# Two loads of a fused attention and feed-forward kernel moved behind a wait on SyncE, and two norms moved ahead

## The chip, the cores and the metric

The kernel runs on one core of one Trainium2 chip. A core has five engines that run their own instruction streams in order: TensorE (PE, with its weight loads PEld), VectorE (DVE), ScalarE (ACT), GpSimd (POOL) and SyncE (SP). Here SP only issues transfers; POOL and ACT issue some too. All transfers run on the core's 16 DMA engines; those issued by SP appear in the profile as queue q1, those by POOL as q0. The metric is the device time of one launch in microseconds (us), lower is better.

## The reference

Cosine attention over 8 batches of 12 heads, 448 tokens, head size 64, and then a feed-forward layer over the joined heads (3584 tokens of 768 features, 2048 inner features):

```python
q_n = q / (np.linalg.norm(q, axis=-1, keepdims=True) + 1e-06)
k_n = k / (np.linalg.norm(k, axis=-1, keepdims=True) + 1e-06)
scores = np.matmul(q_n, k_n.transpose(0, 1, 3, 2)) / tau
scores = scores - np.max(scores, axis=-1, keepdims=True)
attn = np.exp(scores)
attn = attn / (np.sum(attn, axis=-1, keepdims=True) + 1e-09)
attn_out = np.matmul(attn, v)
...
h = x @ w_in
g = np.maximum(0.01 * h, h)
return (g @ w_out).astype(np.float32)
```

tau is 0.1; x is attn_out with the heads of a token side by side. Inputs and the output are float32.

## The kernel before

**Units of work.** Heads are taken two at a time: a *pair* s, numbered 0 to 47 over the whole problem, six pairs to a batch. A *double* j is two pairs (four heads), three to a batch. For each pair the kernel loads q and k (`load_qk`, four transfers on SP: q and k of the first 384 tokens, 192 KB each, and the remaining 64 tokens of each, 32 KB each), squares them on POOL (`squares`, L184), sums the squares on VectorE (`sums`, L195), takes roots on ScalarE (`roots`: a Ln and an Exp, L202 and L203), and scales q and k to bfloat16 `qn` on VectorE (`normalise`: add, reciprocal, two products at L219). `transposes` turns qn into `qkT`: for pairs 0 to 9 by seven matmuls on PE (L233) and a copy on VectorE (L257), from pair 10 on by a DMA transposition issued on SP (L251). `key_tiles` makes the scores of a pair in 128-key tiles on PE (L276) and their exps on ScalarE (`pe`, `pr`, L288). The softmax sums (`totals`) and the products with v (`products`) are matmuls too (L316, and L303 where two doubles share the rest of the keys); `reciprocals` and `scale` turn them into `xT`, the input of the feed-forward part.

**The feed-forward part** goes by chunks c, one to a batch: even chunks have 384 tokens and odd ones 512. `firsts` multiplies by w_in in 16 row tiles m of six matmuls each (L380), and ScalarE applies the leaky relu into `hT` (L387). `visit` multiplies by w_out (`two_groups`, L459): two output halves at once, two passes of 16 steps each, 32 steps n in all, two matmuls to a step; VectorE copies the two finished halves from PSUM to `osb` (L469) and SP stores them. Between the steps, at the numbers in `three` or `four`, a visit issues score tiles of the next batch, so ScalarE's exps run beside w_out's matmuls.

**Order of the work.** The whole order is written out by hand (`tc.manual_schedule()`): each engine executes its instructions in the order in which the Python code records them, and waits where data or a buffer is not ready. So an instruction that waits holds everything recorded behind it on its engine.

**The beginning.** Pairs 0 to 5 (batch 0) are loaded into `raw0` at once. `scaled(s)` at L577 scales pair s + 1, issues a `load_qk` for s = 0, 2 and 3 (pairs 7, 8 and 9; pair 6 is loaded just before, at L542), squares pair s + 3, and has POOL issue bulk transfers (`bulk`): v, four quarters of w_in (768 KB each: two halves of the inner features, and the even and the odd thirds of the model features), and w_out in two column halves, the first in two pieces of 768 KB and the second in four of 384 KB. A tiny copy on POOL (`hold`) makes POOL wait for a scaling before it goes on. Loads from pair 6 on go to the pool `ld` of four buffers, so pairs 6 to 9 have a buffer each, and load 10 waits for pair 6's.

**Pairs 6 to 11** (batch 1) are prepared while chunk 0 goes through w_in and w_out. `norm(s)` is roots, normalise, transposes, the next load, hold and the squares of pair s + 2. `norm(6)` and `norm(7)` are recorded ahead of `firsts(0, ...)`, which holds a table of what is recorded ahead of which m: the sums, norms and transposes of pairs 8 and 9 among them. Pairs 10 and 11 follow inside the first `visit`, at steps 4 and 20 of the first pair of output halves and step 4 of the second.

**PSUM** has eight banks, dealt by `banks`: the least recently used, alone or two side by side. A visit holds two of them for its output halves until VectorE has copied them, and deals the other six in twos to score tiles.

Of the kernel before, what the change touches and what calls it, by code (L numbers as in the profile page):

```python
# [16 lines left out]
def kernel(  # L17
# [10 lines left out]
    nc = tc.nc  # L28
# [89 lines left out]
    def main(x, b, h0, nh):  # L118
        return x[b, h0 : h0 + nh, 0:MAIN].rearrange("h (p t) d -> p h t d", t=3)
# [19 lines left out]
    def load_qk(s):  # L139
        if s >= NSLOT:  # L140
            return
        b, h0 = s // NPAIR, 2 * (s % NPAIR)
        both = ldp.tile([128, 2, 7, D], F32, name="qk")
        nc.sync.dma_start(out=both[:, :, 0:3], in_=main(q, b, h0, 2))
        nc.sync.dma_start(out=both[:, :, 4:7], in_=main(k, b, h0, 2))
        for i, x in enumerate((q, k)):
            nc.sync.dma_start(
                out=both[64 * i : 64 * i + 64, :, 3],
                in_=x[b, h0 : h0 + 2, MAIN:S].rearrange("h p d -> p h d"),
            )  # L150
        raw[s] = (both[:, :, 0:4], both[:, :, 4:7])
# [5 lines left out]
    def load_v(j):  # L157
        if j >= B * NQ:
            return
        b, jj = divmod(j, NQ)  # L160
        vb[j] = vbp.tile([128, 4, 3, D], BF16, name="v_b")
        gp.dma_start(out=vb[j], in_=main(v, b, 4 * jj, 4))  # L162
# [25 lines left out]
    def sums(s, parts=(0, 1)):  # L188
        if s >= NSLOT:
            return  # L190
        if s not in ss:
            ss[s] = smp.tile([128, 14], F32, name="ss")
        for i in parts:
            o = ss[s][:, 0:8] if i == 0 else ss[s][:, 8:14]
            nc.vector.tensor_reduce(  # L195
                o.rearrange("p (h t) -> p h t", h=2), sqs[s][i], axis=AX.X, op=ALU.add
            )
# [6 lines left out]
        if s < 2:  # L204
            nc.scalar.activation(ss[s], ss[s], func=AF.Identity, bias=eps)

    qn = {}

    def normalise(s):
        if s >= NSLOT:  # L210
            return
        r = smp.tile([128, 14], F32, name="r")
        if s >= 2:
            nc.vector.tensor_scalar_add(ss[s], ss[s], 1e-6)  # L214
        nc.vector.reciprocal(r, ss[s])  # L215
        qn[s] = qnp.tile([128, 7, 2, D], BF16, name="qn")
        for x, lo, hi, r0 in ((raw[s][0], 0, 4, 0), (raw[s][1], 4, 7, 8)):
            nt = hi - lo
            nc.vector.tensor_tensor(  # L219
                qn[s][:, lo:hi],  # L220
                x.rearrange("p h t d -> p t h d"),
                r[:, r0 : r0 + 2 * nt].rearrange("p (h t) -> p t h", h=2)
                .unsqueeze(3).to_broadcast([128, nt, 2, D]),
                op=ALU.mult,
            )
# [212 lines left out]
    def two_groups(c, two):  # L438

        po2 = banks(2, ("rows", c, two))
        last = {}
        for n in range(2):
            before, last = last, {}
            for m in range(MT):
                for h in range(2):
                    rows, i = slice(64 * h, 64 * h + 64), h ^ n
                    ts, half = two[i]
                    if n == 1 and m == 0:  # L450
                        tc.add_manual_dep(
                            nc.tensor.nop().ins,
                            before[i].ins.name,
                            mybir.DependencyInfo(
                                mybir.DependencyClass.Sync, mybir.DependencyReason.DATA
                            ),
                            reason="the other rows' products in this bank",
                        )
                    last[i] = nc.tensor.matmul(  # L459
                        out=po2[:, i, :HALF],  # L460
                        lhsT=hT[c][rows, m, ts * 128 : (ts + 1) * 128],
                        rhs=w_out_sb[rows, m, half * HALF : (half + 1) * HALF],
                        start=(n == 0 and m == 0), stop=(n == 1 and m == MT - 1),
                    )
                yield
        for i, (ts, half) in enumerate(two):
            if (c, ts) not in osb:
                osb[c, ts] = osp.tile([128, D_model], F32, name="osb")
            nc.vector.tensor_copy(  # L469
                out=osb[c, ts][:, half * HALF : (half + 1) * HALF], in_=po2[:, i, :HALF]  # L470
            )
            halves_done[c, ts] = halves_done.get((c, ts), 0) + 1
            if halves_done[c, ts] == 2:
                store(osb[c, ts], c, chunk_cols(c)[0] + ts * 128, 0, D_model)
        given_back(("rows", c, two))
# [101 lines left out]
    def scaled(s):  # L577

        if s and s + 2 < NPAIR:
            sums(s + 2, (0,))  # L580
        normalise(s + 1)
        if s != 1 and s < 4:
            load_qk(s + 7 - (s > 1))
        hold(qn[s + 1][:, 6, 0, 0:1])
        squares(s + 3)
        bulk(s)
        if s + 2 < NPAIR:
            sums(s + 2, (1,))
# [108 lines left out]
    def norm(s, transposed=True):  # L697
        if s >= NSLOT:
            return
        roots(s)  # L700
        normalise(s)
        if transposed:
            transposes(s)
        if 9 <= s < 12:
            load_qk(s + 2)
        elif s not in (7, 8):
            load_qk(s + 4)
        hold(qn[s][:, 6, 0, 0:1])
        squares(s + 2)
# [11 lines left out]
    def visit(b, order, norms, between):  # L721


        s0 = (b + 1) * NPAIR
        tiles = [(s0 + p, ki) for p in range(NPAIR) for ki in range(3)]
        key_tiles([(s0 + 1, 3), (s0 + 3, 3)])
        for i, two in enumerate(order):
            after = between[i == len(order) - 1]
            for n, _ in enumerate(two_groups(b, two), 1):
                for _ in range(after.get(n, 0)):  # L730
                    key_tiles([tiles.pop(0)])
                if not tiles and s0 + 5 not in ended:
                    ended.add(s0 + 5)
                    key_tiles([(s0 + 5, 3)])
                if n == 4 and i < norms:
                    norm(s0 + 4 + i)
                if n == 20 and i < norms - (b == 0):
                    sums(s0 + 5 + i)
        assert not tiles

    ended = set()
    three = ({5: 1, 11: 1, 16: 2, 21: 1, 27: 1}, {3: 1, 7: 1, 11: 1, 16: 2, 20: 1})
    four = ({5: 1, 11: 1, 16: 2, 24: 1}, {6: 1, 16: 2})
# [9 lines left out]
            8: [lambda: sums(9)],  # L753
            10: [lambda: norm(9, False), lambda: load_v(3)],
            11: [lambda: transposes(8), lambda: load_v(4)],
            13: [lambda: load_v(5), lambda: load_v_rem(1)],
            14: [lambda: transposes(9), lambda: sums(10)],
        },
    )
    ready = 10  # L760
    for b in range(B):
        tokens = chunk_cols(b)[1] // 128
        if b == B - 1:
            for ts in range(tokens):
                for half in range(2):
                    second(b, ts, half)
            break
        order = [((ts, 0), (ts, 1)) for ts in range(tokens)]
        if b == 0:
            order = [((0, 0), (1, 0)), ((2, 0), (0, 1)), ((1, 1), (2, 1))]  # L770
        visit(b, order, tokens - 1, three if tokens == 3 else four)
        ready += tokens - 1
        attend_batch(b + 1)
        for j in range((b + 2) * NQ, (b + 3) * NQ):
            load_v(j)
        load_v_rem(b + 2)
        s = ready
        between = {0: [lambda s=s: norm(s)], 1: [lambda s=s: sums(s + 1)]}
        if b == 0:
            between = {  # L780
                0: [lambda: sums(13)], 1: [lambda: norm(13), lambda: sums(14)],
                4: [lambda: norm(14), lambda: sums(15)], 7: [lambda: norm(15)],
                13: [lambda: sums(16)],
            }
            ready += 4
        elif tokens == 3:
            between.update({
                4: [lambda s=s: norm(s + 1), lambda s=s: sums(s + 2)],
                7: [lambda s=s: norm(s + 2), lambda s=s: sums(s + 3)],
                10: [lambda s=s: norm(s + 3)], 13: [lambda s=s: sums(s + 4)],  # L790
            })
            ready += 4
        else:
            between.update({
                4: [lambda s=s: norm(s + 1)], 5: [lambda s=s: sums(s + 2)],
                8: [lambda s=s: norm(s + 2)], 12: [lambda s=s: sums(s + 3)],
            })
            ready += 3
        firsts(b + 1, 0, between)
# [35 lines left out]
```

## Time and profile before

| | us |
|---|---|
| runs (median of 3) | 410.01 (409.76 to 410.94) |
| profiled execution, device time | 410.21 |
| its span | 408.4 |
| PE busy | 400.1 (98%) |
| ACT busy | 259.3 (63%) |
| DVE busy | 193.6 (47%) |
| POOL busy | 141.8 (35%) |

The times of the profile are microseconds from the start of its span. The granted clock of TensorE is full in the whole span. By the chain of work that ended last, 90% of the span lies on PE and 8% on transfers. The kernel's stages for batch 0 and chunk 0: attention from the start to about 30 us, w_in from 30.0 to 51.3, the first visit from 51.3 to 72.2, then attention of batch 1.

When transfers of the beginning were issued (their first issue), and when they had landed:

| transfer | issued | landed |
|---|---|---|
| load 8 (pair 8's q and k) | 16.21 | 28.5 |
| load 9 | 18.99 | 34.05 |
| load 10 | 38.38 | 48.2 |
| load 11 | 41.39 | 53.07 |
| w_in, four quarters | 15.45, 19.52, 22.99, 25.90 | 24.85, 30.66, 36.8, 40.4 |
| w_out, last piece | 33.26 | 60.06 |
| qkT of pair 10 | 56.26 | 65.4 |
| qkT of pair 11 | 60.99 | 68.3 |

A landing is the issue plus the time from issue to landing that the view of the DMA issues gives. Where a transfer's packets run and which ones alternate with them is seen in the same view, which counts packets and megabytes of each queue for any stretch.

### The profile page before, as it was taken

The page shows a single profiled execution, that of the slowest core. Times are in us where ns is not written, and L with a number is a line of the kernel's source. Part 1 is how long each engine was busy: PE and PEld are TensorE (multiplying, and loading weights), DVE is VectorE, ACT ScalarE, POOL GpSimd, SP SyncE. Part 2 cuts the span into 40 slices and gives each one's busy share as a digit, 9 for nine tenths or more (in the row PEclk, how much of TensorE's full clock was granted, in tenths as well). Part 3 has the DMA queues.
Part 4 walks back from the last instruction along what each step waited for, and adds up shares of the span by engine and source line. Part 5 has one row for each costly group of instructions (what it writes and reads, how often), then busy time and mean ns, then how long its engine had stood idle before and what let it go on. Part 6 is the DMA issues. An engine that isn't in the chain of part 4 may idle for free.

```text
span 408.4 us, 10108 instructions
## 1 busy us (share of the span) xinstructions
PE 400.1 (98%) x4096; PEld 212.5 (52%) x4096; DVE 193.6 (47%) x412; ACT 259.3 (63%) x448; POOL 141.8 (35%) x216
## 2 busy tenths in 40 slices
PE   7899999999999999999999999999999999999996
PEld 2335655444555655544555555544555555544564
DVE  6887951772644724355553635256262645130021
ACT  4996598455865579645875569745775559844300
POOL 4995473281323422253241614055231530000000
PEclk9999999999999999999999999999999999999999
DMA  8999999595495749378384857486376833210033
GB/s 184 252 220 210 222 191 195 179 204 125 119 212 85 143 90 216 64 116 161 95 205 100 124 134 153 122 116 136 90 192 128 125 75 63 63 41 2 0 77 79
DMA packets 104175, 54.21 MB, mean 133 GB/s; under 512 B 70016, under 2 KB 99072, under 8 KB 104128
## 3 DMA queue, kind: packets, MB, share of 16 engines
q1 hardware_dynamic: 78064, 41.04, 42.6%
q0 software_dynamic: 25216, 12.00, 23.3%
q8 instruction: 32, 0.52, 0.6%
q10 hardware_dynamic: 848, 0.52, 0.4%
q14 instruction: 15, 0.12, 0.1%
HBM read 45.61 MB, written 11.01 MB: 139 GB/s over the span
## 4 chain that ended last, share of the span: by engine, by line
PE 90%; DMA 8%; POOL 1%; SPq 1%; issue 0%; DVE 0%
PE ps L380 36%; PE ps L459 30%; PE ps L316 11%; PE ps L276 7%; PE ps L417 5%; DMA w_in_sb<-in_moe_w_in_dram 3%; DMA qkT<-qn 2%; DMA raw<-in_k_dram 1%; DMA raw<-in_q_dram 1%; PE ps L303 1%; DMA qk<-in_q_dram 1%; POOL sq L184 0%; PE ps L233 0%; POOL v_rem L169 0%; SPq L129 0%; SPq L134 0%
## 5 line engine op out<-in xcount | busy, mean ns | idle before, releaser
L380 PE MATMUL ps<-xT,w_in_sb 128*128 128x384 bf16 (+1 forms) x768 | 148.2, 353 | 0.4 <-DMA w_in_sb<-in_moe_w_in_dram 0.4
L459 PE MATMUL ps<-w_out_sb,hT 64*128 64x384 bf16 x1536 | 142.7, 323 | 0.0
L288 ACT ACTIVATE pe<-ps 128x896 bf16<-128x896 f32 x144 | 123.2, 918 | 20.0 <-PE ps L276 18.0
L387 ACT ACTIVATE hT<-ps 128x384 bf16<-128x384 f32 (+1 forms) x128 | 67.4, 543 | 70.2 <-PE ps L380 69.8
L380 PEld LDWEIGHTS <-w_in_sb 128*128 128x128 bf16 x768 | 74.1, 98 | 72.2 <-issue 4.0
L459 PEld LDWEIGHTS <-hT 64*128 64x128 bf16 x1536 | 73.6, 94 | 54.8 <-issue 3.3
L184 POOL TENSOR_TENSOR sq<-qk 128x512 f32<-128x512 f32 x84 | 77.5, 943 | 15.2 <-DMA qk<-in_k_dram 14.6
L469 DVE COPY osb<-ps 128x384 f32<-128x384 f32 x48 | 24.5, 553 | 77.8 <-PE ps L459 44.6
L276 PE MATMUL ps<-qkT 64*128 64x448 bf16 (+1 forms) x384 | 53.9, 354 | 2.0 <-ACT pe L288 0.9
L195 DVE TENSOR_REDUCE ss<-sq 128x6 f32<-128x384 f32 (+1 forms) x95 | 54.3, 610 | 1.2 <-POOL sq L184 1.0
L516 POOL CAST seen<-qn 128x1 f32<-128x1 bf16 x48 | 9.6, 199 | 130.5 <-DVE qn L219 125.9
L219 DVE TENSOR_TENSOR qn<-qk,r 128x512 bf16<-128x512 f32 x84 | 50.8, 646 | 2.0 <-DVE r L215 0.7
L214 DVE TENSOR_SCALAR ss<-ss 128x14 f32<-128x14 f32 x46 | 10.5, 229 | 66.9 <-ACT ss L203 66.9
L357 DVE TENSOR_TENSOR xT<-ps,rb 128x448 bf16<-128x448 f32 x48 | 27.8, 620 | 20.9 <-ACT rb L336 20.7
L162 POOL DMA_DIRECT2D v_b<-in_v_dram x24 | 18.8, 784 | 54.2 <-PE ps L316 54.2
L316 PE MATMUL ps<-pe,v_b 128*32 128x448 bf16 x576 | 31.9, 353 | 0.0
L276 PEld LDWEIGHTS <-qkT 64*128 64x128 bf16 (+1 forms) x384 | 16.5, 96 | 22.1 <-issue 8.8
L335 ACT ACTIVATE rb<-ps 128x448 f32<-128x448 f32 x24 | 12.9, 538 | 22.2 <-PE ps L316 21.2
L423 DVE COPY osb<-ps 128x384 f32<-128x384 f32 (+1 forms) x9 | 4.6, 513 | 36.6 <-issue 22.6
L288 ACT ACTIVATE pr<-ps 128x896 bf16<-128x896 f32 x24 | 21.3, 921 | 0.2 <-PE ps L276 0.2
L316 PEld LDWEIGHTS <-v_b 128*32 128x32 bf16 x576 | 15.0, 97 | 12.1 <-issue 0.6
L417 PE MATMUL ps<-w_out_sb,hT 128*128 128x384 bf16 (+1 forms) x144 | 21.0, 308 | 0.0
(51 smaller groups left out, 196.0 us busy)
## 6 DMA issues: line engine op xcount, KB each, us to landing
qk<-in_q_dram SPq DMA_DIRECT2D x42, 192.0 KB, 3.3
qk<-in_k_dram SPq DMA_DIRECT2D x42, 192.0 KB, 3.3
out_dram<-osb SPq DMA_DIRECT2D x30, 192.0 KB, 3.0
v_b<-in_v_dram POOLq DMA_DIRECT2D x24, 192.0 KB, 4.8
out_dram<-osb SPq DMA_DIRECT2D x12, 384.0 KB, 2.6
w_in_sb<-in_moe_w_in_dram POOLq DMA_DIRECT2D x4, 768.0 KB, 12.5
w_out_sb<-in_moe_w_out_dram POOLq DMA_DIRECT2D x2, 768.0 KB, 21.7
w_out_sb<-in_moe_w_out_dram POOLq DMA_DIRECT2D x4, 384.0 KB, 25.6
```

Source lines behind the costliest of these rows:

```text
L184: eng.tensor_tensor(sq, x, x, op=ALU.mult)
L195: nc.vector.tensor_reduce(o.rearrange("p (h t) -> p h t", h=2), sqs[s][i], axis=AX.X, op=ALU.add)
L219: nc.vector.tensor_tensor(qn[s][:, lo:hi], x.rearrange("p h t d -> p t h d"), r[:, r0 : r0 + 2 * nt].rearrange("p (h t) -> p t h", h=2) .u ...
L276: nc.tensor.matmul(out=out[:, a, :S], lhsT=x[rows, c0:c1], rhs=x[rows, 0:S], start=True, stop=True,)
L288: nc.scalar.activation(out=dst, in_=sc[:, :, :S], func=AF.Exp, scale=inv_tau)
L316: nc.tensor.matmul(out=x[32 * g : 32 * g + 32, :S], lhsT=weights(g, ki) if ki < 3 else rem(g), rhs=pe[s][:, ki, a, :] if ki < 3 else pr[j] ...
L357: nc.vector.tensor_tensor(xT[m][:, 2 * jj + e, half * S : (half + 1) * S], pos.pop((j, e))[:, :S], rbs[j], op=ALU.mult,)
L380: nc.tensor.matmul(out=pm[:, :n], lhsT=w_in_sb[:, kt, m * 128 : (m + 1) * 128], rhs=xT[c // 2][:, kt, c0 : c0 + n], start=(kt == 0), stop= ...
L387: nc.scalar.activation(out=hT[c][:, m, :n], in_=pms.pop((c, m))[:, :n], func=AF.Prelu, alpha=0.01)
L417: nc.tensor.matmul(out=po2[:, :n], lhsT=hT[c][:, m, ts * 128 : (ts + 1) * 128], rhs=w_out_sb[:, m, lo : lo + n], start=(m == 0), stop=(m = ...
L459: last[i] = nc.tensor.matmul(out=po2[:, i, :HALF], lhsT=hT[c][rows, m, ts * 128 : (ts + 1) * 128], rhs=w_out_sb[rows, m, half * HALF : (ha ...
L469: nc.vector.tensor_copy(out=osb[c, ts][:, half * HALF : (half + 1) * HALF], in_=po2[:, i, :HALF])
```

## The change

Four things are moved, and nothing is added to the arithmetic.

1. `load_qk(8)` and `load_qk(9)` leave `scaled(2)` and `scaled(3)` and stand in `scaled(4)`, behind an empty instruction on SP that waits for the second product of `normalise(5)`. The helper `behind` records such a wait; the one that `two_groups` already had on PE uses it now too, unchanged.
2. `transposes(9)` is recorded ahead of m = 13 in place of m = 14.
3. `norm(10)` is recorded ahead of m = 15 of `firsts(0, ...)` in place of step 4 of the visit's first pair of output halves.
4. `sums(11)` is recorded at step 16 in place of 20, and `norm(11)` at step 26 of the first pair of output halves in place of step 4 of the second. The other visits get the same steps as before, by a table.

The order of instructions on each engine: on PE the seven transposes of pair 9 pass six L380; on ScalarE the roots of pair 10 pass one hT and two pr, and the roots of pair 11 one exp; on VectorE the scaling of pair 11 passes the two copies of the first output halves. The orders on POOL and on SP are the same as before, except for the empty instruction on SP.

```diff
-    qn = {}
+    qn, scalings = {}, {}
+
+    def behind(eng, ins, why):
+
+        tc.add_manual_dep(
+            eng.nop().ins, ins.ins.name,
+            mybir.DependencyInfo(mybir.DependencyClass.Sync, mybir.DependencyReason.DATA),
+            reason=why,
+        )
...
-            nc.vector.tensor_tensor(
+            scalings[s] = nc.vector.tensor_tensor(
                 qn[s][:, lo:hi],
...
                     if n == 1 and m == 0:
-                        tc.add_manual_dep(
...
+                        behind(nc.tensor, before[i], "the other rows' products in this bank")
...
         normalise(s + 1)
-        if s != 1 and s < 4:
-            load_qk(s + 7 - (s > 1))
+        if s == 0:
+            load_qk(7)
+        elif s == 4:
+            behind(nc.sync, scalings[5], "weights first")
+            load_qk(8)
+            load_qk(9)
         hold(qn[s + 1][:, 6, 0, 0:1])
...
-                if n == 4 and i < norms:
-                    norm(s0 + 4 + i)
-                if n == 20 and i < norms - (b == 0):
-                    sums(s0 + 5 + i)
+                for fn in norms.get((i, n), ()):
+                    fn()
...
-            13: [lambda: load_v(5), lambda: load_v_rem(1)],
-            14: [lambda: transposes(9), lambda: sums(10)],
+            13: [lambda: load_v(5), lambda: load_v_rem(1), lambda: transposes(9)],
+            14: [lambda: sums(10)],
+            15: [lambda: norm(10)],
...
-        visit(b, order, tokens - 1, three if tokens == 3 else four)
+        norms = {(0, 16): [lambda: sums(11)], (0, 26): [lambda: norm(11)]}
+        if b:
+            norms = {}
+            for i in range(tokens - 1):
+                norms[i, 4] = [lambda s=ready + i: norm(s)]
+                norms[i, 20] = [lambda s=ready + i + 1: sums(s)]
+        visit(b, order, norms, three if tokens == 3 else four)
```

## The prediction

> **What bounds the kernel now.** First the waits of TensorE between 24 and 75 us, in total, times and longest:
>
> ```profile
> PE ps L380 <- DMA w_in_sb<-in_moe_w_in_dram: 0.4, 1, 0.4
> PE ps L276 <- DMA qkT<-qn: 0.3, 1, 0.3
> ```
>
> Two transfers stop TensorE. The timeline (start, length, engine, group, idle before it) gives their places:
>
> ```profile
> 30.01 0.34 PE L380 MATMUL ps<-xT,w_in_sb 128*128 128x384 bf16 x1
> 30.70 0.66 PE L380 MATMUL ps<-xT,w_in_sb 128*128 128x384 bf16 x3 [0.36 <-DMA w_in_sb<-in_moe_w_in_dram]
> 65.44 0.36 PE L276 MATMUL ps<-qkT 64*128 64x448 bf16 x2 [0.32 <-DMA qkT<-qn]
> ```
>
> Idle time understates such a wait, since matmuls are pipelined; starts are better. The second L380 starts 0.69 after the first where the stage runs at 0.16 (96 in 15.71): 0.53 us lost on the second quarter of w_in. For qkT I compare the same stage of two batches, stretches of 51.36 to 72.19 and 146.91 to 167.00:
>
> ```profile
> 51.36:72.19 20.83, 20.44 (x248) 11.09 (x254) 6.66 (x14) 18.91 (x26) 10.98 (x15) 1.00 1.29 186
> 146.91:167.00 20.09, 20.09 (x249) 11.26 (x253) 7.22 (x16) 18.91 (x26) 4.79 (x7) 1.00 0.59 121
> ```
>
> The first number is length, the second PE busy: visit 0 is 0.74 longer than visit 2. Before 30 us ScalarE is the limit (busy 9.55 and 9.82 of the 10 us from 10 and from 20) and the loads gate nothing there; after 72 us PE meets no wait that the list shows. So the change can win at most 0.53 + 0.74 = 1.27 us, 0.31%.
>
> **Part 1: loads 8 and 9 behind a wait on SP.** Nothing is added but one empty instruction. SP's next work, load 10, waits for the scaling of pair 6 until 38.38 (a wait of 16.1 us in SP's list), so SP has room: pair 5 is scaled by 27.45 (L219 at 26.29, 1.16), the eight issues at about 0.6 end by 32.3. POOL's weight queue (q0) is not passed or held. In the present run loads 8 and 9 are issued from 16.21 and 18.99, and their packets alternate one for one with q0's:
>
> ```profile
> q0 software_dynamic: 158, 0.32, 89.4%
> q1 hardware_dynamic: 143, 0.08, 19.2%
> ...
> q0 software_dynamic: 320, 0.24, 75.9%
> q1 hardware_dynamic: 316, 0.23, 46.6%
> ```
>
> (packets, MB, share; first two lines 20 to 22 us, beside w_in; the others 42 to 44, beside w_out.) A w_in quarter of 384 packets lands 3.6 us after the one before when it is alone (36.8, 40.4), so 9.4 ns a packet; 158 such packets leave 0.5 us of two for q1's 143, some 3.5 ns each. The second quarter lands at 30.66 with about 1,000 q1 packets interleaved ahead of it, so without them between 27 and 28; it is needed at 30.17. Gain 0.53, with at least 2 us of cover.
>
> Price: loads 8 and 9 land later. From first issue to last landing, the loads of before take 12.3 (load 8), 15.1 (9), 9.8 (10) and 11.7 us (11). Load 9 is now issued from 29.9, so it lands between 41.6 (11.7) and 45.0 (15.1). I take 44.0: the first packet moves 3.6 us after the issue, as load 10's did (38.38, then 4 packets until 42.0), so at 31.1; w_in is through at about 35.6, some 380 packets later, and the remaining 1,150 of the two loads' 1,536 go at 160 per us beside w_out until 42.7, plus 1.3 to landing as for loads 10 and 11. Load 8 by the same count lands at 39.3; POOL wants it at 38.1, and waits. Load 10 follows load 9 in the queue: 48.7 (47.7 to 49.9), against 48.2 now.
>
> **Part 2: the transposes of pair 9 one chunk earlier.** This costs PE nothing in work (7 matmuls, 0.39 either way), but they move ahead of six L380, and what they read is barely ready now:
>
> ```profile
> 41.66 1.04 POOL L184 TENSOR_TENSOR sq<-qk 128x512 f32<-128x512 f32 x1
> 45.43 1.14 DVE L195 TENSOR_REDUCE ss<-sq 128x8 f32<-128x512 f32 x2
> 47.67 1.16 DVE L219 TENSOR_TENSOR qn<-qk,r 128x512 bf16<-128x512 f32 x2
> 48.86 0.55 PE L233 MATMUL ps<-id,qn 128*128 128x128 bf16 x7
> ```
>
> These are pair 9's squares (first half), sums, scaling and transposes. The scaling ends at 48.83; the chain has the transposes at 49.02. The new place is 49.02 − 6 × 0.1625 − 0.53 = 47.5, done at 47.9 if the data were there. It isn't: if all of VectorE's work moved up by the same 0.53, the scaling would end at 48.30. With load 9 at 44.0 the squares end at 45.85 (1.82 both), and by the rows above the scaling ends 2.83 after the squares (second sum 0.57, then 48.83 − 46.57 = 2.26), at 48.65. Three transposes remain, 0.2: PE is through at 48.85, 0.95 late. Bounds: 0.6 (load 9 before 43.6) and 1.95 (at 45.0). PE takes matmuls in order, so all of w_in's last chunks wait behind it. This gives back more than part 1 gains; without part 1's 0.53 the wait would be 0.4 and the sum the same.
>
> **Part 3: pair 10's norm ahead of the visit.** The roots (0.55 of ScalarE) stand before the last hT and the two pr instead of behind them. They need sums(10), which end 2.76 after load 10 lands (48.37, 51.13): 51.45 by my 48.7, and ScalarE comes free at 51.35 (hT at 50.42 + 0.49, plus PE's 0.42). So almost no wait; the last hT ends about 52.6, and the bank it frees is wanted by the scores of the visit's fifth step at 53.1. Cover 0.5; past it each us costs one. Pair 10's transposition is issued near 54.0 instead of 56.26 and takes 9.1 at most as now: 63.1, wanted at 65.4. Gain 0.48 (start 65.44 against 64.96 by the steps of 0.081).
>
> **Part 4: pair 11's norm at the 26th step.** On ScalarE this passes one exp only (0.82): the roots start at 58.2 to 58.7 with PE's delay, against 58.63, the transposition at 60.5 against 60.99. Load 12 is now issued 2 to 3 us sooner, so less stands ahead of it; at 7.3 us as now it lands at 67.8, wanted at 68.1. Gain the other 0.26. Against it, VectorE evicts the first two output halves (2 × 0.51) behind the norm, until 61.4 instead of 59.37; the dealing order gives their banks to the second pair's 16th step, on PE at 61.12 + 0.42 = 61.54. It just fits; I take 0, with 0.5 as the bad end.
>
> **Sum**: −0.53 + 0.95 − 0.74 = −0.3 us (bounds −0.7 and +0.7 with load 9's). The profiled execution has a span of 408.4 within 410.21; it becomes 408.1 within 409.9. The median of the runs, 410.01, becomes **409.7**.
>
> **The rivals.**
> *Load 9 lands late (slower).* Place: PE stands at L233 for pair 9 (L219 late). The break-even is a wait of 1.27, load 9 at 44.3, only 0.3 past my estimate; each us more costs one. At 45.0, the longest latency of before, 410.7; load 10 at 49.9 then holds the roots on ScalarE until 52.65, hidden behind PE's own delay. Slower by 1.2 us needs 45.6. For it: q1 gets one packet per w_in packet, and both loads now queue right behind each other; against: w_in is through sooner. The Trainium skill (DMA: Bandwidth & Descriptors, Rules for kernel authors) advises to issue a DMA early, compute, and wait on it late. This change does the reverse for these two loads, and by that rule this rival would be the outcome; the trace agrees as far as load 8 lies landed for 10 us (28.5 to 38.6) now.
> *The whole gain (faster).* Pair 9 is scaled by 47.5 and nothing else waits: −1.27, 408.7. For it: the scaling of pair 7 takes 2.63 (38.70) instead of 1.16 beside POOL's squares(8), and a later load 8 would part them. Against: then squares(8) themselves, until 41.1, set sums(8), now at 41.24.
> *A later wait takes the gain.* The evictions of part 4 come 0.5 late, or the last piece of w_out (lands 60.06, read at 60.47) is pushed back by pair 10's transposition, whose packets now share its last 2 us: +0.5 on my sum, 410.2.
> *The change doesn't free w_in*: the second quarter stays late. Then 0.53 is lost, but the wait in part 2 shrinks by as much: 409.7 again.
>
> **How the numbers follow.** Forecast (with the last rival) 0.46, late load 0.31, later wait 0.1, whole gain 0.13. The measurement can tell about 0.3% (1.2 us) from no change. Faster by that needs nearly the whole cap: 0.14 with the edge of the forecast. Slower by that is two thirds of the late-load case, since its queue carries load 10 along, and a little of the later waits: 0.24. The rest is 0.62. The range leaves out the top of the late case and the edge of the whole gain: 408.8 to 411.2; the likeliest case alone has 409.3 to 410.7.
>
> **What would show it.** Right: no PE wait on w_in at 30; an idle of PE at pair 9's transposes near 48, released by DVE L219; POOL idle before squares(8) and (9) for DMA qk; no PE wait on qkT; visit 0 near 20.1 us. Wrong: no idle at L233 (then the whole gain), or one of over 2 us, or ScalarE idle before L202 near 51 with PE held behind it at L276.

## The result, and the profile after

The changed kernel took 412.44 us (median of 9 runs, 411.19 to 413.96) against 410.01 us before (9 runs, 409.70 to 411.15). The ratio is 1.0057, with a 95% interval of 1.0035 to 1.0079: slower, by about 2.4 us where 0.3 us less was forecast, and above the top of the range (411.2). The nine runs fall in two groups: five between 411.19 and 412.44, with a mean granted clock of 1.000, and four between 413.29 and 413.96, with 0.996. The profiled execution is one of the first group: 411.59 us, span 409.8.

The changed kernel's lines from L207 on carry other numbers: pair 9's scaling is L227 (L219 before), the transposes L241 (L233), scores L284 (L276), w_in L388 (L380), hT L395 (L387), w_out L460 (L459), the DMA transposition L259 (L251). "Before" is the kernel before throughout.

Waits of TensorE between 24 and 75 us, in the changed kernel (total, times, longest):

```profile
PE ps L241 <- DVE qn L227: 2.1, 1, 2.1
```

Both waits of before, for w_in and for qkT, are gone from that list, and one new wait stands there that is larger than what they were worth. The timeline of the changed kernel (start, length, engine, group, idle before it and what ended it), first TensorE:

```profile
30.18 0.82 PE L388 MATMUL ps<-xT,w_in_sb 128*128 128x384 bf16 x4
...
45.73 1.95 PE L388 MATMUL ps<-xT,w_in_sb 128*128 128x384 bf16 x11
49.76 0.81 PE L241 MATMUL ps<-id,qn 128*128 128x128 bf16 x7 [2.08 <-DVE qn L227]
```

At 30.18 four L388 run without a gap, so the 0.53 us of the second quarter of w_in is won. At 47.68 TensorE has done what stands before pair 9's transposes and then does nothing for 2.08 us. What it waits for begins on SP, whose timeline in the changed kernel has the four issues of load 9:

```profile
29.99 0.60 SPq L144 DMA_DIRECT2D qk<-in_q_dram  x1
30.64 0.47 SPq L145 DMA_DIRECT2D qk<-in_k_dram  x1
31.15 2.60 SPq L147 DMA_DIRECT2D qk<-in_q_dram  x1
33.80 1.24 SPq L147 DMA_DIRECT2D qk<-in_k_dram  x1
```

The timeline of POOL and VectorE in the changed kernel has the squares of pairs 8 and 9, and the second pair's sums and scaling:

```profile
40.60 1.83 POOL L184 TENSOR_TENSOR sq<-qk 128x512 f32<-128x512 f32 x2 [2.35 <-DMA qk<-in_k_dram]
45.49 1.82 POOL L184 TENSOR_TENSOR sq<-qk 128x512 f32<-128x512 f32 x2 [2.94 <-DMA qk<-in_k_dram]
46.56 1.34 DVE L195 TENSOR_REDUCE ss<-sq 128x8 f32<-128x512 f32 x2 [0.76 <-POOL sq L184]
49.01 1.16 DVE L227 TENSOR_TENSOR qn<-qk,r 128x512 bf16<-128x512 f32 x2
```

The four issues of load 9 run from 29.99 to 35.04; the last landed 11.5 us after 33.80, at 45.3. POOL stands idle for load 8 (until 40.60) and then for load 9 (until 45.49), VectorE for POOL, and the scaling ends at 50.17: 1.34 later than before, and TensorE wants it 1.5 sooner. Loads 8, 9, 10 and 11 landed at 40.4, 45.3, 50.25 and 55.2: a train, 5 us to a pair. The DMA view says why it is no faster. Packets, MB and share of each queue of the changed kernel from 34 to 36 us, and from 38 to 40:

```profile
q0 software_dynamic: 165, 0.33, 86.3%
q1 hardware_dynamic: 164, 0.11, 23.7%
...
q0 software_dynamic: 339, 0.26, 82.6%
q1 hardware_dynamic: 345, 0.17, 42.5%
```

The loads' queue (q1) gets as many packets as POOL's (q0) and no more: 82 per us while q0 carries packets of 2 KB, some 170 when they are of 768 bytes. A pair has 768 packets, so at 155 per us it takes 5 us.

The visit itself, from 53.49, where the chain of work that ended last reaches its first scores (51.36 before; stretch, length, then busy time and instructions of PE, PEld, DVE, ACT and POOL, granted clock, DMA share, GB/s):

```profile
53.49:73.58 20.09, 20.09 (x249) 11.24 (x254) 6.50 (x14) 18.62 (x24) 10.57 (x15) 1.00 1.12 174
```

It is 20.09 long, as long as visit 2, where nothing waits: the 0.74 us is won too. The books of the profiled execution: the visit starts 2.13 later than before (53.49 against 51.36) and is 0.74 shorter, so 1.4 us are lost, and the span grew by 1.4 (408.4 to 409.8). Of the 2.13, 0.17 lie ahead of w_in, whose first matmul starts at 30.18 instead of 30.01. That much is no effect of the change: among the profiles below, two kernels whose order up to there is that of before start w_in at 29.80 (parts 3 and 4 alone) and at 31.05 (part 4 alone). What follows the visit takes 336.3 us in every profile.

### The profile page after: what moved, and what is told of

It is laid out like the page before. It is cut to its first block, busy times and chain, and to the rows that moved or that the text cites. A ratio compares the mean times of both kernels' runs of the same rounds, so it can differ in the third digit from the quotient of the medians.

```text
span 409.8 us, 10098 instructions
## 1 busy us (share of the span) xinstructions
PE 400.0 (98%) x4086; PEld 212.9 (52%) x4096; DVE 191.9 (47%) x412; ACT 259.0 (63%) x448; POOL 140.3 (34%) x216
## 3 DMA queue, kind: packets, MB, share of 16 engines
q1 hardware_dynamic: 78064, 41.04, 43.2%
## 4 chain that ended last, share of the span: by engine, by line
PE 87%; DMA 6%; DVE 2%; SPq 2%; issue 1%; POOL 1%; ACT 0%; POOLq 0%
PE ps L388 32%; PE ps L460 31%; PE ps L324 10%; PE ps L284 7%; PE ps L425 5%; DMA qk<-in_k_dram 3%; DMA raw<-in_k_dram 2%; PE ps L311 1%; DVE qn L227 1%; DMA raw<-in_q_dram 1%; SPq L147 1%; POOL sq L184 1%; DMA qk<-in_q_dram 1%; DVE ss L195 0%; DVE ss L222 0%
## 5 line engine op out<-in xcount | busy, mean ns | idle before, releaser
L388 PE MATMUL ps<-xT,w_in_sb 128*128 128x384 bf16 (+1 forms) x760 | 147.6, 352 | 0.4
L460 PE MATMUL ps<-w_out_sb,hT 64*128 64x384 bf16 x1536 | 142.8, 323 | 0.0
L395 ACT ACTIVATE hT<-ps 128x384 bf16<-128x384 f32 (+1 forms) x128 | 67.2, 543 | 70.0 <-PE ps L388 69.5
L388 PEld LDWEIGHTS <-w_in_sb 128*128 128x128 bf16 x768 | 74.1, 98 | 71.7 <-issue 4.0
L460 PEld LDWEIGHTS <-hT 64*128 64x128 bf16 x1536 | 73.6, 94 | 54.9 <-issue 3.3
L184 POOL TENSOR_TENSOR sq<-qk 128x512 f32<-128x512 f32 x84 | 76.6, 933 | 19.1 <-DMA qk<-in_k_dram 18.4
L284 PE MATMUL ps<-qkT 64*128 64x448 bf16 (+1 forms) x384 | 53.9, 354 | 1.8 <-ACT pe L296 0.9
L227 DVE TENSOR_TENSOR qn<-qk,r 128x512 bf16<-128x512 f32 x84 | 49.0, 625 | 2.0 <-DVE r L223 0.6
L284 PEld LDWEIGHTS <-qkT 64*128 64x128 bf16 (+1 forms) x384 | 16.5, 96 | 21.1 <-issue 8.8
```

Of the source, the lines that this page charges most:

```text
L184: eng.tensor_tensor(sq, x, x, op=ALU.mult)
L227: scalings[s] = nc.vector.tensor_tensor(qn[s][:, lo:hi], x.rearrange("p h t d -> p t h d"), r[:, r0 : r0 + 2 * nt].rearrange("p (h t) -> p ...
L284: nc.tensor.matmul(out=out[:, a, :S], lhsT=x[rows, c0:c1], rhs=x[rows, 0:S], start=True, stop=True,)
L388: nc.tensor.matmul(out=pm[:, :n], lhsT=w_in_sb[:, kt, m * 128 : (m + 1) * 128], rhs=xT[c // 2][:, kt, c0 : c0 + n], start=(kt == 0), stop= ...
L395: nc.scalar.activation(out=hT[c][:, m, :n], in_=pms.pop((c, m))[:, :n], func=AF.Prelu, alpha=0.01)
L460: last[i] = nc.tensor.matmul(out=po2[:, i, :HALF], lhsT=hT[c][rows, m, ts * 128 : (ts + 1) * 128], rhs=w_out_sb[rows, m, half * HALF : (ha ...
```

## The experiments

The twelve experiments ran on three chips, four to a chip in the order below, each beside runs of the kernel before on the same chip: 410.49 us on the first (18 runs), 409.84 on the second (12) and 410.13 on the third (35). Ratios are against those, with 95% intervals.

### Parts 2 to 4 without part 1

```diff
-        if s == 0:
-            load_qk(7)
-        elif s == 4:
-            behind(nc.sync, scalings[5], "weights first")
-            load_qk(8)
-            load_qk(9)
+        if s != 1 and s < 4:
+            load_qk(s + 7 - (s > 1))
```

> Loads 8 and 9 back in their old places, the rest of the change kept. Theory A (load 9 lands at 45.4 and PE stands at pair 9's transposes for its scaling): load 9 lands near 34 again, pair 9 is scaled by 48.8, and PE idles about 0.7 us at the transposes instead of 2.1; the wait on w_in (0.5 us lost) returns and the 0.74 us of the visit stay won: 409.9, all runs within 1 us of each other. Theory B (the reordering costs by itself: the roots of pair 10 ahead of the last hT, the scaling of pair 11 ahead of the evictions): still near 412.

Measured: 411.7 us (411.15 to 412.02), 1.0030 [1.0018, 1.0041]. The wait for pair 9's scaling shrank as theory A has it, to 0.38, but the time hardly did. TensorE's timeline shows a wait that no theory named:

```profile
48.44 0.81 PE L241 MATMUL ps<-id,qn 128*128 128x128 bf16 x7 [0.38 <-DVE qn L227]
69.80 0.55 PE L284 MATMUL ps<-qkT 64*128 64x448 bf16 x4 [1.19 <-DMA qkT<-qn]
```

Pair 11's qkT was issued sooner than before (60.70 against 60.99) and landed later, at 69.75 instead of 68.3. So the late load 9 is one cause and not the only one. Theory B named this time, but not this place: TensorE's list has no wait behind the last hT or behind the copies of the output halves. What moves pair 11's transposition is parts 3 and 4, which are taken alone below.

### Part 2 taken back

```diff
-            13: [lambda: load_v(5), lambda: load_v_rem(1), lambda: transposes(9)],
-            14: [lambda: sums(10)],
+            13: [lambda: load_v(5), lambda: load_v_rem(1)],
+            14: [lambda: transposes(9), lambda: sums(10)],
```

> The transposes of pair 9 back ahead of m = 14; loads 8 and 9 stay behind the wait, the norms stay early. Theory A: pair 9 is scaled at 50.2 as in the changed kernel, PE comes to the transposes one chunk (0.98 us) later, so it idles 1.1 instead of 2.1 and the time falls by 1.0: span 408.8, time about 410.5, with fewer runs above 413. If the place of the transposes is the whole cause: no idle at L241, 409. Theory B: no change, 412.

Measured: 411.22 us (410.21 to 412.65, 11 runs), 1.0015 [1.0001, 1.0030], the smallest loss of any version with the train of loads, and near the 0.5 us over the kernel before that theory A expected. The wait for the scaling is 0.83 in place of 2.08 (1.1 was expected). Now the other edge of the change shows, the roots of pair 10 on ScalarE ahead of the last hT:

```profile
53.99 0.36 PE L284 MATMUL ps<-qkT 64*128 64x448 bf16 x2 [0.53 <-ACT hT L395]
```

So the earlier place of the transposes turns lateness of the data into idle time of TensorE; it doesn't make the data late.

### The two loads behind an earlier scaling

```diff
-        elif s == 4:
-            behind(nc.sync, scalings[5], "weights first")
+        elif s == 3:
+            behind(nc.sync, scalings[4], "weights first")
```

> SyncE waits for pair 4's scaling (24.0) in place of pair 5's (27.6), the rest of the change kept. Theory A: loads 8 and 9 land 1.5 to 3 us sooner (load 9 at 42.5 to 44), PE idles 0.5 to 1.2 us at pair 9's transposes, no wait on w_in at 30: 409.3 to 410. If instead the loads can't get through before w_in has landed wherever they are issued: load 9 lands less than 0.7 us sooner, idle over 1.5, 411. Theory B: 412.

Measured: 411.79 us (411.29 to 412.54), 1.0037 [1.0023, 1.0051]. The last issue of load 9 was at 28.78 instead of 33.80, five us sooner, and it landed at 43.4 instead of 45.3, two sooner: the queue sets the landing more than the issue does. The wait at the transposes is 0.3, less than the 0.5 to 1.2 expected, but 1.5 us appear at the scores of pair 11 (qkT issued at 60.07, landed 9.35 later). The expected 409.3 to 410 was a miss, by the same second wait as without part 1.

### The idle time filled

Nine matmuls on constant data (2.1 us) stand before pair 9's transposes; the rest is the changed kernel.

```diff
-        tp = transposed()
+        bank = banks(1)
+        if s == 9:
+            for i in range(9):
+                nc.tensor.matmul(
+                    out=bank, lhsT=warm[:, :128], rhs=warm, start=(i == 0), stop=(i == 8)
+                )
+        tp = bank.bitcast(BF16)[:, : 7 * 128].rearrange("p (t c) -> p t c", c=128)
```

> The changed kernel with nine matmuls on constants (9 x 0.216 = 1.9 us) in front of pair 9's transposes, into the bank that the transposes then overwrite, so that PE works where it stood idle. Theory C (the runs of the changed kernel near 413.5, all with a mean clock of 0.996, are those in which TensorE's clock is lowered after the idle of 2.1 us): span within 0.3 of the changed kernel's 409.8, clock 1.0 in every run, all runs between 411.0 and 412.2. Theory D (those runs come from the transfers): still some four of nine above 413.

Measured: 411.83 us (411.49 to 412.19), 1.0034 [1.0022, 1.0046]. With 2.1 us of matmuls added the time is that of the changed kernel's first group, so those us were free. None of its 6 runs has a clock under 0.999, where 4 of 9 of the changed kernel had 0.996.

### Part 1 alone

The order on all engines is that of before, except that loads 8 and 9 are behind the wait for the sixth pair's scaling:

```diff
-        if s != 1 and s < 4:
-            load_qk(s + 7 - (s > 1))
+        if s == 0:
+            load_qk(7)
+        elif s == 4:
+            behind(nc.sync, scalings[5], "weights first")
+            load_qk(8)
+            load_qk(9)
```

> Only part 1: loads 8 and 9 behind the wait on pair 5's scaling, transposes and norms in the order of before. Theory A (load 9 late, pair 9 scaled near 50): PE idles 0.8 to 1.2 us at L241, and pair 10, whose load follows at 50.3, is transposed late as well, so PE waits again at qkT: 411 to 411.7. If the late loads cost nothing without the moved transposes: 409.5.

Measured: 411.48 us (410.54 to 412.27), 1.0037 [1.0023, 1.0051], as expected. The wait at the transposes in their old place:

```profile
50.27 0.81 PE L241 MATMUL ps<-id,qn 128*128 128x128 bf16 x7 [0.97 <-DVE qn L227]
```

The expected second wait, at pair 10's qkT, didn't come, so the time was right partly by luck. The span of the profiled execution is 0.9 above before, but 0.8 of this lies ahead of w_in (30.82 against 30.01), where profiles of kernels alike up to there differ as much. From w_in to the end of the visit this profile is only 0.1 longer than before: no wait for w_in, the wait of 0.97, and a visit that begins late and is 0.75 shorter. The medians differ by 1.6. So the loss of part 1 alone is shown by the times; this profile shows the late load but not where most of the 1.6 us go.

### Parts 3 and 4 alone

Here and in part 4 alone, the lines taken out are the order of before, written with the change's table.

```diff
+            15: [lambda: norm(10)],
...
-        norms = {(0, 4): [lambda: norm(10)], (0, 20): [lambda: sums(11)], (1, 4): [lambda: norm(11)]}
+        norms = {(0, 16): [lambda: sums(11)], (0, 26): [lambda: norm(11)]}
```

> Only parts 3 and 4: norms of pairs 10 and 11 early, loads and transposes of before. Theory E (found in the first runs: with pair 10's transposition and load 12 issued sooner, their packets push those of v back, and pair 11's transposition, though issued sooner, shares the engines with v and lands near 69.7 in place of 68.3): no wait at qkT of pair 10, but 1.5 to 2 us at qkT of pair 11, span near 409.6, time 411 to 411.7. If the norms win what the prediction gave them (0.74): 409.3.

Measured: 411.63 us (411.38 to 412.93), 1.0045 [1.0032, 1.0058], as theory E expected. The two moves meant to shorten the visit lengthen it when nothing delays TensorE before it. The profile is of the slowest of the six runs (412.93, span 411.2), in which the clock falls as well after the wait, as the last section shows. In TensorE's timeline:

```profile
69.57 0.55 PE L284 MATMUL ps<-qkT 64*128 64x448 bf16 x4 [2.00 <-DMA qkT<-qn]
```

### Part 1 alone, behind the earlier scaling

The edit is that of part 1 alone, with `scalings[4]` at s = 3.

> Part 1 alone with the wait on pair 4's scaling: load 9 lands near 43.4, pair 9 is scaled in time for transposes at their old place, no wait on w_in. Theory F (what PE gains at 30 us it gives back at the next wait for a transfer, since qkT of pair 10 lands when the transfers allow): wait at qkT of pair 10 near 0.8 in place of 0.3, time within 0.3 of before. If the 0.53 us stay won: 0.5 below before.

Measured: 412.12 us (410.18 to 412.88, 7 runs), 1.0044 [1.0028, 1.0061]: a miss. The wait for the scaling is gone, and two others stand in its place, first the last piece of w_out (issued at 32.97, landed 28.9 later, at 61.9), then qkT:

```profile
61.89 0.81 PE L460 MATMUL ps<-w_out_sb,hT 64*128 64x384 bf16 x7 [1.12 <-DMA w_out_sb<-in_moe_w_out_dram]
70.34 0.55 PE L284 MATMUL ps<-qkT 64*128 64x448 bf16 x4 [1.12 <-DMA qkT<-qn]
```

In this profile w_out's last piece is later than in any other. That the loads' packets made it late is not shown: with loads 8 and 9 both behind a wait it landed between 59.9 (the changed kernel) and 61.9, in the other kernels between 60.0 and 60.5. Only here did TensorE come for it sooner than it landed.

### The changed kernel again

> The changed kernel once more, on the chip of this call. Theory A and C: near 1.0057 of before, part of its runs about 2 us above the rest with a mean clock below 1.0, and the idle of PE at L241 over 2 us. If the high runs belong to the first chip alone: all runs within 1 us.

Measured: 412.76 us (410.97 to 414.01), 1.0064 [1.0041, 1.0087], with three of six runs between 413.54 and 414.01 at a clock of 0.996. Both groups are there again. This time the profile is of a run of the upper group (span 412.2). TensorE's wait in its timeline:

```profile
50.74 0.97 PE L241 MATMUL ps<-id,qn 128*128 128x128 bf16 x7 [2.17 <-DVE qn L227]
```

The windows behind it in the same profile, of TensorE alone (stretch, length, PE busy and instructions, then the granted clock, DMA share, GB/s):

```profile
50.00:52.00 2.00, 1.26 (x9) 0.68 1.22 231
52.00:54.00 2.00, 2.00 (x8) 0.50 1.28 209
54.00:56.00 2.00, 2.00 (x15) 0.97 1.31 201
```

After an idle time of 2.17 us TensorE gets half its clock from about 50.7 to 54.1, for 3.4 us, which takes 1.7 us. In the first group's profile the idle time is 2.08 and the clock is full in the same windows:

```profile
50.00:52.00 2.00, 1.93 (x16) 1.00 1.23 231
52.00:54.00 2.00, 2.00 (x20) 1.00 1.29 201
54.00:56.00 2.00, 2.00 (x26) 1.00 1.32 202
```

### Part 4 alone

```diff
-        norms = {(0, 4): [lambda: norm(10)], (0, 20): [lambda: sums(11)], (1, 4): [lambda: norm(11)]}
+        norms = {(0, 4): [lambda: norm(10)], (0, 16): [lambda: sums(11)], (0, 26): [lambda: norm(11)]}
```

> Only part 4 of the change (norm(11) at step 26 of its group instead of step 4 of the next), with loads 8 and 9, transposes(9) and norm(10) where the kernel before has them. Theory E (what makes qkT(11) late is pair 10's transposition and load 12, sent sooner by part 3, sliding v's packets into qkT(11)'s time): those stay where they were, so qkT(11), issued 0.5 us or more sooner, lands by 68.3 and the wait of 0.74 at its scores shrinks to 0 to 0.5: 409.3 to 410.1 us. Rival H (the transfers before 70 us are full, and any transposition issued sooner there lands at 69 or later all the same): a wait of 1 to 2 us at L276's line, 411 to 411.7 us.

Measured: 410.17 us (409.49 to 411.25, 12 runs), 1.0003 [0.9993, 1.0013]: no change. But the reason is not quite theory E's. The transposition was issued at 62.25, 9.9 us after the visit's start, where before it was 9.6: SP was still at load 12's issues until 62.14. Without part 3, part 4 doesn't bring the transposition forward. In this one profile the visit is 20.37 long, 0.46 less than before; the median of the runs doesn't show that.

### Load 12 behind pair 11's transposition

In `norm`, with the order of before otherwise:

```diff
-        if 9 <= s < 12:
-            load_qk(s + 2)
+        if s == 11:
+            load_qk(12)
+            load_qk(13)
+        elif s == 9:
+            load_qk(11)
...
-        squares(s + 2)
+        if s == 11:
+            squares(12)
+        if s != 10:
+            squares(s + 2)
```

> The kernel before with load 12 (and pair 12's squares) behind pair 11's transposition instead of in norm(10), nothing else moved. Theory E: between 57 and 62 us load 12 no longer takes turns with v's packets, so qkT(11) lands at 66 to 68.1 and the wait of 0.74 at its scores goes or halves: 409.2 to 409.8 us. Rival H: it lands where it did (68 to 69.5): 409.8 to 411.5 us.

Measured: 409.93 us (409.23 to 410.34, 11 runs), 0.9991 [0.9979, 1.0002]. Pair 11's transposition took 5.3 us to land instead of 7.3 (66.8), TensorE has no wait there, and the profiled visit is 20.09 long, 0.74 shorter than before. That is the wait that theory E expected to go. The time, 409.93, is a little above its 409.2 to 409.8; the interval includes no change, and also the 0.9982 that 0.74 us would give.

### Parts 3 and 4, with load 12 behind pair 11's transposition

The two edits above together.

> Parts 3 and 4 of the change (norm(10) ahead of the visit, norm(11) at step 26) with load 12 and pair 12's squares behind pair 11's transposition. Those parts with load 12 sent from norm(10) took 411.63 us. Theory E: without load 12 in its way, qkT(11), issued near 59.7, lands by 67.5, no wait at its scores: 409.0 to 409.8 us. If pair 10's transposition alone is what slides v's packets: lands near 69, wait of 1 to 1.5 us: 410.8 to 411.6 us.

Measured: 409.99 us (409.56 to 411.15, 11 runs), 1.0003 [0.9992, 1.0013], where the same norms with load 12 in its place had 1.0045 [1.0032, 1.0058]. So load 12 is what makes them slow (pair 12's squares, moved with it, ran on POOL from 66.23 without this edit, after POOL's last issue for v, which ended at 59.6). The queues from 66 to 67 us (packets, MB, share), with load 12 in its place:

```profile
q0 software_dynamic: 323, 0.09, 81.9%
q1 hardware_dynamic: 316, 0.08, 61.5%
```

And with load 12 later, in the same stretch:

```profile
q1 hardware_dynamic: 317, 0.11, 125.6%
q0 software_dynamic: 26, 0.00, 4.9%
```

Load 12 takes the turns of v's packets (q0): from 60 to 62 us q0 moves 219 packets with load 12 in its place and 436 with it later. So v is still being moved when pair 11's transposition runs, and takes every second turn from it. With load 12 later, v is all but through by 65 (68 of q0's packets in the next us), and the transposition lands 8.0 us after its issue at 60.13 instead of 9.9 us after 59.67. The wait of 2.00 is gone. What was to be won is not: it lands at 68.1, the scores that read it start at 68.18, 0.3 later in the visit than with load 12 alone moved, and the wait for w_in is there as before.

### Load 9 alone behind the wait

```diff
+        elif s == 2:
+            load_qk(8)
         elif s == 4:
             behind(nc.sync, scalings[5], "weights first")
-            load_qk(8)
             load_qk(9)
```

Parts 2 to 4 are taken back.

> Of part 1 only load 9 is put behind the wait for the sixth pair's scaling; load 8 stays in its old step, and parts 2 to 4 are taken back. Theory A (the two loads behind the wait run as a train, and load 9 is late because load 8 goes ahead of it there): load 9 lands at 42.5 to 44.2, the wait at pair 9's transposes is under 0.4, and the wait for w_in is between 0 and 0.53: 409.3 to 410.1 us. Rival: the wait itself, not the train, makes load 9 late (45 or later): a wait of 1 us at the transposes, 410.8 to 411.6 us.

Measured: 410.16 us (409.57 to 411.39, 11 runs), 1.0004 [0.9995, 1.0014]: no change, by theory A. Load 9's last transfer was issued at 29.62 and landed 11.8 later, at 41.4, a good us sooner than the earliest that was expected. POOL has no idle time before pair 9's squares and TensorE none before its transposes:

```profile
41.71 1.82 POOL L184 TENSOR_TENSOR sq<-qk 128x512 f32<-128x512 f32 x2
...
48.91 0.55 PE L241 MATMUL ps<-id,qn 128*128 128x128 bf16 x7
```

Same wait, same place on SP, one load in place of two, and the 0.37% that part 1 alone costs is gone. The wait for w_in is 0.2 in its list, 0.4 before.

## Why the prediction was wrong

**The step that failed** is in part 1: "I take 44.0" for the landing of load 9, and with it in part 2 "PE is through at 48.85, 0.95 late". The mechanism was right and the size was off. Load 9 landed at 45.3, past even the upper bound of 45.0, which was the longest latency of before (15.1) put on the first issue (29.9). What happens from there on goes by the prediction's own steps: both squares end 1.82 after they start, the scaling 2.83 after that, three transposes 0.2 later; with squares from 45.49 this is 50.34, and 47.9 was wanted, so 2.44 late. The sum −0.53 + 2.44 − 0.74 is +1.2, a span of 409.6; it measured 409.8, with 0.17 of it ahead of w_in.

**Why 44.0 was too early.** The count had 380 packets sent by 35.6 and then 160 per us. The queue counts show about 335 by 35.6 and the slow rate of 82 per us until 36 or 37, since w_in's packets of 2 KB were not through: its last quarter landed at 38.0, where the count had 35.6. So 1,536 packets were reached at 43.2 instead of 42.7. The last landing came 2.1 us behind that, where 1.3 had been put. The eight issues also took longer, until 35.04 and not 32.3, but the run behind the earlier scaling shows that this weighs less: there the last issue came 5 us sooner and the landing 2. The longest latency of before was no upper bound for the second of two loads that start together late.

**The gains** of 0.53 and 0.74 both came in the profiled execution: no wait for w_in at 30, none for qkT, a visit of 20.09. But the working of the second was wrong. "Load 12 is now issued 2 to 3 us sooner, so less stands ahead of it; at 7.3 us as now it lands at 67.8": with parts 3 and 4 alone it took 9.9 us and landed at 69.57, since load 12 sent sooner pushes v's packets into its way. In the changed kernel this didn't show: the transposition, issued at 62.17, landed at 68.4, and TensorE, 2.1 us late, wanted it at 69.8. So the gain of 0.74 that the forecast counted on was there only beside a delay larger than the gain.

**The smaller terms.** The copies of the first output halves ahead of their use fit, as put: no wait at L460. The roots of pair 10 had a cover of 0.5, and no wait in the changed kernel. With part 2 taken back the cover was passed, and TensorE waited 0.53 behind the last hT; the runs of the norms without part 1 have no such wait.

**The rivals.** The late load 9 is what happened, at its place and price: it gave +1 us for a landing at 45.3. The Trainium skill's rule that stood beside it (DMA: Bandwidth & Descriptors, Rules for kernel authors: issue early, wait late) held here: with load 9 alone moved nothing was won over the early issue, and with both moved 0.37% was lost. Load 12 is the other way round: sent sooner, it cost what sending it later took away again (1.0045 against 1.0003). A later wait, the third rival, came too, in versions where TensorE was less late: once at w_out's last piece, as it says, and several times at pair 11's qkT, which it does not name. The change did free w_in, so the last rival is out.

**What no case had** is the clock. It accounts for 1.7 of the some 2 us by which the upper group of runs lies above the first (medians 413.66 and 411.59), and with it for the median lying 1 us over what the waits alone give. That the half clock follows the idle time is shown by the windows of two profiles and supported by the run with the idle time filled; which runs get it is not settled. One of 18 runs of the kernel before on the first chip (411.51) and one of 11 with load 9 alone behind the wait (410.53) have a mean clock of 0.996 too, though the profiles of these two kernels show no wait over 0.5 us from w_in to the end of the visit; those runs themselves have no profile.

No version was faster than before by more than the measurement tells. The one with load 12 later comes nearest, at 0.9991 [0.9979, 1.0002]. Load 9 alone behind the wait, together with the early norms and the later load 12, was not run, so whether 0.53 and 0.74 can be had at once stays open.

## What to carry to other kernels

Where two queues take turns packet by packet, a transfer's landing is set by how many packets of its own queue stand before it and by the size of the other queue's packets (here 82 per us beside 2 KB, some 170 beside 768 bytes), so count the whole train behind a new wait, not one transfer with the latency it had elsewhere. A transfer moved earlier takes turns from another that is read later: before crediting the move, list who else is on the queues until the last one is through, and test each part alone, since a delay in one part can hide the loss in the next. If data may be late at all, leave the consumer where other work of its engine covers it.

## What the runs showed of the hardware

**The clock of TensorE halves after an idle time of 2 us, sometimes.** Of the profiled executions with such an idle time, the one of 2.17 us (the changed kernel again) and the one of 2.00 (parts 3 and 4 alone) show it; the changed kernel's first profile, with 2.08, doesn't. In the windows of parts 3 and 4 alone, TensorE starts again at 69.57, and the half clock comes about 1 us later and lasts 3.4 us, from 70.6 to 74.0:

```profile
70.50:71.00 0.50, 0.50 (x6) 0.63 1.07 405
...
73.50:74.00 0.50, 0.50 (x6) 0.50 0.00 0
74.00:74.50 0.50, 0.50 (x10) 0.95 0.00 0
```

The Trainium skill (TensorE: Matmul & The Clock Gate, Part 1) puts half rate after at least one idle window of some 3.4 us, and says that the window runs free of the kernel. The length of 3.4 us agrees with that, and so does the fact that only some of the runs show it. The idle time needed does not: 2.00 and 2.17 us were enough.

**An issue on SP is not always 0.6 us.** The seventh of eight transfers issued in a row took 2.60 (at 31.15 in the changed kernel), and a load's issues held pair 11's transposition until 62.14 in the run of part 4 alone.

**One and the same DMA transposition** took 5.3, 7.3, 8.0 and 9.9 us from issue to landing in four kernels that move the same data and differ in when they issue it.
